# Fifteen input loads of an attention-and-feed-forward kernel, issued by ScalarE instead of SyncE

## The chip, the cores and the metric

The kernel runs on one core of a Trainium2 chip. The core has a matrix engine (TensorE, PE in the profile, with its weight loads as PEld), a vector engine (VectorE, DVE), a scalar engine (ScalarE, ACT), a general engine (GpSimd, POOL) and an engine that issues transfers and synchronizes (SyncE, SP). Each works through a queue of its own in order, and instructions wait for each other by semaphores. Sixteen DMA engines move data between HBM and the on-chip memory SBUF; TensorE's results land in PSUM, which has eight banks. The metric is the device time of one execution in microseconds; less is better.

## The reference

Eight batches of attention with 8 heads, 576 tokens and a head width of 64, of the kind that multiplies k by v first, so that no matrix of tokens by tokens arises; then a feed-forward layer with a product in the middle. All inputs and the output are in float32.

```python
q_s = softmax(q over the head width)
k_s = softmax(k over the 576 tokens)
kv  = einsum('bhsd,bhse->bhde', k_s, v)
x   = einsum('bhsd,bhde->bhse', q_s, kv)       # to (4608, 512)
h   = (x @ w1) * (x @ w2)                      # 512 -> 1024
out = (h @ w3) @ w_out                         # 1024 -> 1024 -> 512
```

In both softmaxes the greatest value is subtracted before the exponential, and 1e-9 is added to the sum.

## The kernel before

A class `Plan` holds some hundreds of named steps. A step has an engine (or several to choose from), a function that emits its instructions, and its needs. The text `ORDER` (from L83) lists the names by hand, and the steps are emitted in that sequence: each engine's queue is the sequence of its own steps in `ORDER`, and a letter behind a name (/A, /D, /P) picks ACT, DVE or POOL where there is a choice. Semaphores are set by what a step reads and overwrites. So `ORDER` says only what stands ahead of what on one engine; between engines the data decide.

At the start w3 @ w_out is folded to one matrix W3O of 1024 x 512 (L398). Then the work runs over batches b = 0 to 7 of attention and chunks c = 0 to 8 of the feed-forward layer, and the steps of several of them are interleaved so that PE has products of one while the other engines prepare the next. The steps for attention, with the lines at which the profile shows them:

- `q.b`, `k.b`, `v.b`: the loads (L358), from batch 2 on one transfer of 1152 KB each, all in float32. Each of the three has two buffers, which the batches use in turn, so that a load has to wait for the last step that reads the older batch in its buffer: the exponential of k two batches before for `k.b`, the exponential of q for `q.b`, the cast of v for `v.b`. The loads of batches 0 and 1 and of the weights are issued by POOL (two of q by SP); those of batches 2 to 7 by SP.
- `qmx` (DVE, L547: the maximum), `qsub` (POOL or DVE, L553), `qexp` (ACT, L561, into eq), `qsm` (DVE, L579: the sum), `qeps` and `qrc` (L585 and L590), `qn` (POOL, L597, into en): the softmax of q, in two parts p = 0 and 1 of each batch.
- `qd.b.p` (SP, L631): DMA transposes of a part of en to qT, as PE needs the head width in the partitions. Part 0 has 8 blocks, part 1 has 10.
- `kmi`, `kmx`, `cb` (ACT and DVE, L435 to L468): the maximum of k over the tokens; `ksub` (L475) and `kexp` (ACT, L483, into ek).
- `vc` (ACT, L275): the cast of v to float16. `kv` (PE, L501, into the banks pkv): k times v; `kv2` (DVE, L521 to L531): its division by the sums.
- `xm` and `xt` (PE, L649): q times kv, of the main 512 tokens and of the tails; `xs` and `xts` (mostly ACT, L279): their results, scaled and cast to the tiles x and xtail.

For a chunk: `up` (PE, L809, into pab: w1 and w2 side by side), `bs` (ACT, L275: one of them cast to bsb), `ab` (DVE, L834: the product), `down` (PE, L842, into po), `os` (ACT, L275, to outs) and `st` (SP, L869 and L969: the store). Chunk 8 collects the tails of all batches. Chunks 5 to 8 of the upward and 3 to 7 of the downward product are made with seven products in place of eight (steps um and dm, L904 and L945), with sums made by DVE and POOL.

On SP, loads, transposes and stores thus share one queue, in the sequence of `ORDER`; a step waits there for its needs, and everything behind it waits as well. An engine that issues a DMA goes on as soon as the issue is done; the transfer then runs by itself, and signals a semaphore when it lands. ACT issues only one transfer before the change, a part of the last store.

Of the kernel before, what the change touches and what calls it, by code (L numbers as in the profile page):

```python
# [101 lines left out]
up.1.1.1.3 qn.2.1/P kexp.2.0 down.1.0.0 down.1.0 kmi.3 kmx.3.0 bs.1.1.1/A ab.1.1.1 vc.2.0/A qd.2.0 xt.1 bs.1.1.2/A
ksub.2.1/P vc.2.1/A kmx.3.1 cbt.3 kexp.2.1 qsub.3.1/P xts.1.0/A ab.1.1.2 xts.1.1/A q.4 qexp.3.1 ws.2.0/P ab.1.1.0 kv.2
kv2.2 down.1.1.0 down.1.1 qd.2.1 xm.2.1 qmx.3.0 qsub.3.0/P os.1.0/A bs.1.1.3/A xs.2.1.1/A qmx.4.1 qsub.4.1/P xm.2.0
xs.2.0.1/A xt.2 qsm.3.1 xs.2.0.0/A xs.2.1.0/A cbx.3 xts.2.1/A v.3 down.1.2.0 up.0.1.1.3 up.1.2.0.0 bs.2.0.0/A qmx.4.0
xts.2.0/D up.0.2.0.0 up.1.2.0.1 qsub.4.0/P up.0.2.0.1 up.1.2.0.2 k.4 v.4 qexp.3.0 cb.3 ksub.3.1/P qsm.3.0 os.1.1/A
# [5 lines left out]
qrc.4.0 qn.4.0/P cbt.4 cbx.4 kv.3 ab.2.0.7 qexp.5.0 down.2.0 kv2.3 xm.3.0 xs.3.0.1/A xs.3.0.0/A xm.3.1 xs.3.1.0/A xt.3
xts.3.1/A xts.3.0/A cb.4 ksub.4.1/P k.5 qmx.6.1 down.2.1 xs.3.1.1/D qsm.5.0 vc.4.1/A os.2.1/A ksub.4.0/P up.1.3.0.0
up.0.3.0.0 qmx.6.0 qsub.6.0/P bs.3.0.0/A ab.3.0.0 os.2.0/A qeps.5.0/A qrc.5.0 st.1.1 qmx.5.1 qsub.5.1/P up.1.3.0.1
up.0.3.0.1 up.1.3.0.2 up.0.3.0.2 bs.3.0.1/A qd.4.1 up.1.3.0.3 up.0.3.0.3 up.1.3.0.4 ab.3.0.1 v.5 kmi.5 kmx.5.0 kmx.5.1
cbt.5 st.2.1 kexp.4.0 vc.4.0/A kexp.4.1 kv.4 bs.3.0.2/A qsub.6.1/P kv2.4 bs.3.0.4/A up.0.3.0.4 ab.3.0.4 down.2.2
bs.3.0.3/A ab.3.0.2 qexp.5.1 qd.4.0 cbx.5 qsm.5.1 qexp.6.0 xm.4.1 xs.4.1.0/A xm.4.0 xs.4.0.1/A qn.5.0/P xs.4.0.0/A
up.1.3.0.5 ws.3.1/D up.0.3.0.5 up.1.3.0.6 up.0.3.0.6 v.6 qeps.5.1/A wt.4/D ws.4.0/D os.2.2/A wt.3/D ws.3.0/D qrc.5.1
qn.5.1/P qexp.6.1 cb.5 ksub.5.0/P bs.3.0.6/A ab.3.0.6 k.6 vc.5.0/A xs.4.1.1/A up.1.3.0.7 up.0.3.0.7 q.7 qsm.6.1
ab.3.0.3 bs.3.0.5/A vc.6.0/A up.1.4.0.0 ab.3.0.5 up.0.4.0.0 up.1.4.0.1 st.1.3 bs.3.0.7/A ksub.5.1/P up.0.4.0.1 qsm.6.0  # L120
kmi.6 bs.4.0.1/A bs.4.0.0/A kmx.6.0 st.2.0 vc.6.1/A down.2.3 qeps.6.1/A os.2.3/A qrc.6.1 kmx.6.1 up.1.4.0.2 qd.5.0
# [8 lines left out]
ue.5.1.2/A k.7 xs.6.0.1/A ad.4.2/D um.5.2.6 ue.5.2.2/A ad.4.4/D um.5.1.7 ws.4.1/D um.5.2.7 ue.5.2.7/A um.5.0.7  # L130
um.5.1.5 ue.5.1.4/A ue.5.1.7/A ad.4.3/D um.5.2.2 uc.5.2.1 qeps.7.0/A um.5.0.1 xs.6.0.0/A um.5.2.4 uc.5.2.3 qrc.7.0
ue.5.0.7/A um.5.1.3 uc.5.1.4/P ab.5.1.1 ue.5.0.1/A um.5.2.5 ue.5.2.4/A um.5.1.2 uc.5.1.1 ab.5.2.0/P st.3.0 st.2.2
um.5.0.2 uc.5.0.1 um.5.0.4 um.5.0.6 ue.5.0.2/A uc.5.0.3 uc.5.2.4/P um.5.3.7 xd.6.3/P qn.7.0/P dm.4.1 kmi.7 kmx.7.0
um.5.3.1 ue.5.3.7/A um.5.1.4 uc.5.1.3 ab.5.1.0/P kmx.7.1 ue.5.3.1/A um.5.3.2 uc.5.3.1 de.4.1/A um.5.0.5 ue.5.0.4/A
# [1048 lines left out]
```

## Time and profile before

| | |
|---|---|
| median of 3 runs | 227.42 us (227.4 to 227.42) |
| profiled execution | 227.57 us |
| its span, first to last instruction | 225.8 us |
| granted TensorE clock | 1.000 |
| PE busy | 219.3 us, 97% |
| PE's weight loads busy | 150.6 us, 67% |
| DVE busy | 203.9 us, 90% |
| ACT busy | 161.6 us, 72% |
| POOL busy | 141.1 us, 62% |
| moved by DMA | 46.89 MB, 208 GB/s over the span |

A busy share says how much of the span an engine worked, not what it cost. Here PE is the engine to watch: where it is never idle, work on the others lies beside it and costs nothing until it comes too late for a product. For that, the rows of the instructions in order of time are read, with their start and length: how long before its use a tile was ready. A wait is put down to the semaphore that came last. A DMA has two times: the issue, in which the issuing engine's queue is held, and the landing. In the tables of DMA queues q1 is SP's ring, q0 is POOL's.

### The profile page before, as it was taken

The page shows a single profiled execution, that of the slowest core. Times are in us where ns is not written, and L with a number is a line of the kernel's source. Part 1 is how long each engine was busy: PE and PEld are TensorE (multiplying, and loading weights), DVE is VectorE, ACT ScalarE, POOL GpSimd, SP SyncE. Part 2 cuts the span into 40 slices and gives each one's busy share as a digit, 9 for nine tenths or more (in the row PEclk, how much of TensorE's full clock was granted, in tenths as well). Part 3 has the DMA queues.
Part 4 walks back from the last instruction along what each step waited for, and adds up shares of the span by engine and source line. Part 5 has one row for each costly group of instructions (what it writes and reads, how often), then busy time and mean ns, then how long its engine had stood idle before and what let it go on. Part 6 is the DMA issues. An engine that isn't in the chain of part 4 may idle for free.

```text
span 225.8 us, 5662 instructions
## 1 busy us (share of the span) xinstructions
PE 219.3 (97%) x2250; PEld 150.6 (67%) x2250; DVE 203.9 (90%) x363; ACT 161.6 (72%) x280; POOL 141.1 (62%) x96
## 2 busy tenths in 40 slices
PE   7998999999999999999999999999999999999994
PEld 2454658865886544444444657888888888888853
DVE  2989879989998999999998999999999988899881
ACT  2556476785859997899999986988995846453511
POOL 8344405787999799999679928297474055602320
PEclk9999999999999999999999999999999999999999
DMA  6999999999999999999969186482193040044343
GB/s 222 214 273 248 294 227 251 367 387 300 277 276 369 388 324 357 187 312 280 385 164 296 22 134 212 128 221 96 32 200 64 3 107 34 3 124 157 89 145 139
DMA packets 38042, 46.89 MB, mean 208 GB/s; under 512 B 18048, under 2 KB 21504, under 8 KB 38016
## 3 DMA queue, kind: packets, MB, share of 16 engines
q1 hardware_dynamic: 32144, 35.92, 56.5%
q0 software_dynamic: 5728, 10.55, 20.0%
q8 instruction: 17, 0.28, 0.5%
q10 hardware_dynamic: 144, 0.07, 0.1%
q14 instruction: 9, 0.07, 0.1%
HBM read 38.80 MB, written 9.44 MB: 214 GB/s over the span
## 4 chain that ended last, share of the span: by engine, by line
PE 67%; DMA 20%; DVE 8%; ACT 2%; POOL 1%; issue 1%; POOLq 0%; ACTq 0%; SPq 0%; DVEq 0%
PE pab L809 19%; PE uA L904 12%; PE dA L945 8%; DMA w1sb<-in_moe_w_dram 8%; PE uB L904 6%; PE po L842 6%; DMA w<-in_moe_w_dram 5%; DMA wosb<-in_moe_w_out_dram 5%; PE dB L945 4%; DMA q<-in_q_dram 3%; PE uC L904 3%; PE po L857 3%; PE dC L945 2%; DVE qm L547 2%; PE pkv L501 2%; DVE qr L579 2%
## 5 line engine op out<-in xcount | busy, mean ns | idle before, releaser
L809 PE MATMUL pab<-x,w2sb 128*128 128x256 f16 (+1 forms) x224 | 40.6, 318 | 0.0
L809 PE MATMUL pab<-x,w1sb 128*128 128x256 f16 (+1 forms) x224 | 40.6, 318 | 0.0
L597 POOL TENSOR_TENSOR en<-eq,qr 128x1024 f16<-128x1024 f16 (+1 forms) x14 | 29.7, 2126 | 8.3 <-DVE k L475 4.3
L809 PEld LDWEIGHTS <-w2sb 128*128 128x128 f16 x224 | 21.6, 98 | 13.4 <-issue 1.0
L809 PEld LDWEIGHTS <-w1sb 128*128 128x128 f16 x224 | 21.7, 98 | 13.0 <-issue 0.2
L553 POOL TENSOR_TENSOR q<-q,qm 128x1280 f32<-128x1280 f32 (+1 forms) x13 | 27.7, 2143 | 2.2 <-DVE qm L547 1.8
L475 POOL TENSOR_TENSOR k<-k,cb 128x1152 f32<-128x1152 f32 x10 | 26.2, 2626 | 2.5 <-DVE k L475 2.5
L904 PEld LDWEIGHTS <-w 128*128 128x128 f16 x256 | 25.0, 98 | 3.3
L834 DVE TENSOR_TENSOR ab<-pab,bsb 128x512 f16<-128x512 f32 x40 | 25.9, 672 | 0.2
L275 ACT CAST bsb<-pab 128x512 f16<-128x512 f32 x40 | 23.2, 594 | 3.8 <-PE pab L809 3.6
L561 ACT ACTIVATE eq<-q 128x1024 f16<-128x1024 f32 (+2 forms) x16 | 18.7, 1169 | 8.2 <-DVE q L553 7.6
L547 DVE TENSOR_REDUCE qm<-q 128x16 f32<-128x1024 f32 (+2 forms) x16 | 21.2, 1333 | 3.7 <-DMA q<-in_q_dram 3.7
L842 PE MATMUL po<-W3O,ab 128*128 128x512 f16 x96 | 22.7, 380 | 0.0
L579 DVE TENSOR_REDUCE qr<-eq 128x16 f32<-128x1024 f16 (+2 forms) x16 | 21.4, 1339 | 0.0
L483 ACT ACTIVATE ek<-k 128x1152 f16<-128x1152 f32 x16 | 18.8, 1172 | 3.3 <-DVE k L475 2.4
L279 ACT ACTIVATE x<-xm 128x512 f16<-128x512 f32 x30 | 16.4, 605 | 3.6 <-PE xm L649 1.9
L904 PE MATMUL uA<-v,w 128*128 128x256 f16 x128 | 17.9, 273 | 0.0
L275 ACT COPY v<-uA 128x512 f32<-128x512 f32 x24 | 14.1, 601 | 4.8 <-PE uA L904 4.3
L945 PEld LDWEIGHTS <-k 128*128 128x128 f16 x160 | 15.5, 98 | 2.1
L883 POOL TENSOR_TENSOR k<-ab,k 128x1024 f16<-128x1024 f16 x3 | 6.4, 2130 | 16.4 <-DVE bsb L883 10.0
L275 ACT CAST v<-v 128x1152 f16<-128x1152 f32 x14 | 16.3, 1170 | 0.0
L398 PE MATMUL pf<-wosb,aux 128*128 128x512 f16 x64 | 15.6, 379 | 0.4 <-DMA wosb<-in_moe_w_out_dram 0.4
(140 smaller groups left out, 464.7 us busy)
## 6 DMA issues: line engine op xcount, KB each, us to landing
q<-in_q_dram SPq DMA_DIRECT2D x6, 1152.0 KB, 6.5
k<-in_k_dram SPq DMA_DIRECT2D x6, 1152.0 KB, 8.9
v<-in_v_dram SPq DMA_DIRECT2D x6, 1152.0 KB, 8.8
out_dram<-outs SPq DMA_DIRECT2D x23, 256.0 KB, 3.5
...
```

The costliest lines, as they stand in the source:

```text
L275: return [(nc.scalar.copy if eng == "ACT" else engine[eng].tensor_copy)(out=out, in_=in_)]
L475: return [engine[eng].tensor_tensor(out=kb[:, two(hp), :, :], in0=kb[:, two(hp), :, :], in1=st["cb", b][:, two(hp), None, :].broadcast_to( ...
L483: nc.scalar.activation(out=st["ek", b][:, hp, :, :].rearrange("p j (i d) -> p i j d", i=2), in_=kb[:, two(hp), :, :], func=AF.Exp)
L547: dve.tensor_reduce(out=st["qm", b][:, hs, j], in_=qb[:, hs, j, :], axis=AX.X, op=ALU.max, **({"negate": True} if (b, p) in FEXP else {}))
L553: return [engine[eng].tensor_tensor(out=qb[:, hs, j, :], in0=qb[:, hs, j, :], in1=st["qm", b][:, hs, j, None].broadcast_to([P, nh, n, D]), ...
L579: dve.tensor_reduce(out=st["qr", b][(slice(None), *part(p))], in_=st["eq", b, p], axis=AX.X, op=ALU.add)
L597: return [engine[eng].tensor_tensor(out=st["en", b][:, j, hs, :].rearrange("p j h d -> p h j d"), in0=st["eq", b, p], in1=st["qr", b][:, h ...
L809: nc.tensor.matmul(st["p", one, c, sub, u][:, a * (t1 - t0):(a + 1) * (t1 - t0)], lhsT=w[:, ct, fb * P:(fb + 1) * P], rhs=x()[:, ct, t0:t1 ...
L834: dve.tensor_tensor(out=st["ab", c][:, nf * u:nf * u + nf, t0:t1], in0=cut(st["p", 0, c, sub, u]), in1=cut(st["bsb", c, sub, u]), op=ALU.mult)
L842: nc.tensor.matmul(st["po", c, tb], lhsT=st["ab", c][:, ft, tb * P:(tb + 1) * P], rhs=W3O[:, ft, :], start=(ft == 0), stop=(ft == N_FT - 1))
L904: nc.tensor.matmul(t[:, u, :], lhsT=w[:, k0 + kk, fb * P:(fb + 1) * P], rhs=r[:, kk, :], start=(p in (1, 2, 7) and u == 0 and kk == 0), st ...
L945: nc.tensor.matmul(t[:, i, :], lhsT=l[:, f, i * P:(i + 1) * P], rhs=r[:, f, :], start=(p in (1, 2, 7) and i == 0 and f == 0), stop=(i == 1 ...
```

## The change

The loads of q, k and v of batches 3 to 7 are issued by ACT instead of SP. A list of names picks them; the loads of batch 2, the transposes and the stores stay on SP. In `ORDER` the moved loads get places among ACT's steps, about where SP came to issue them, and a few steps of SP (qd.2.0, qd.2.1, qd.4.0, qd.4.1, qd.6.1, st.1.1, st.2.2, st.3.0) stand a little earlier. The computing instructions of ACT, PE, DVE and POOL stand in the same sequence as before. What a load waits for is the same as before; only that the wait now stands in ACT's queue.

```diff
@@ ORDER
-up.0.0.1.3 ab.0.0.2 k.3 ab.0.1.0 bs.0.1.3/A ab.0.1.3 ws.1.1/D up.0.0.1.2 bs.0.1.2/A ab.0.1.2 down.0.0.0 qmx.2.0
+up.0.0.1.3 ab.0.0.2 ab.0.1.0 bs.0.1.3/A ab.0.1.3 ws.1.1/D up.0.0.1.2 bs.0.1.2/A ab.0.1.2 down.0.0.0 qmx.2.0 down.0.0
...
+    ALOAD = [('q', 3), ('q', 4), ('q', 5), ('q', 6), ('q', 7), ('k', 3), ('k', 4), ('k', 5), ('k', 6), ('k', 7), ('v', 3), ('v', 4), ('v', 5), ('v', 6), ('v', 7)]
...
     for b in range(2, B):
         for n in "kqv":
-            load((n, b), "SP")
+            load((n, b), "ACT" if (n, b) in ALOAD else "SP")
```

Three places show what that makes of the queues. In the names, q32_1, k32_1 and v32_1 are the second buffers of the inputs (batches 1, 3, 5) and q32_0, k32_0 and v32_0 the first ones. First SP's queue between 42 and 57 us, from q.2 to v.2, before and after:

```order
L358 DMA q32_0_71<-in_q_dram 128x4x576
L358 DMA k32_0_69<-in_k_dram 128x4x576
L631 DMA_TRANSPOSE qT_710<-en_688 128x8x128
L358 DMA k32_1_70<-in_k_dram 128x4x576
L358 DMA q32_1_72<-in_q_dram 128x4x576
L631 DMA_TRANSPOSE qT_710<-en_688 128x10x128
L358 DMA v32_0_73<-in_v_dram 128x4x576
```

```order
L359 DMA q32_0_71<-in_q_dram 128x4x576
L359 DMA k32_0_69<-in_k_dram 128x4x576
L632 DMA_TRANSPOSE qT_710<-en_688 128x8x128
L632 DMA_TRANSPOSE qT_710<-en_688 128x10x128
L359 DMA v32_0_73<-in_v_dram 128x4x576
```

k.3 and q.3 stood between the two transposes of batch 1 and are gone from there. Second, ACT's queue at the casts of v of batch 1, around 46 to 53 us, before and after:

```order
L275 CAST bsb_686<-pab_676 128x512
L275 CAST bsb_713<-pab_541 128x512
L275 CAST bsb_737<-pab_716 128x512
L275 CAST bsb_750<-pab_666 128x512
L275 CAST v16_1_76<-v32_1_74 128x2x9x64 x2
L561 ACTIVATE eq_775<-q32_1_72 128x1280
L585 ACTIVATE qr_636<-qr_636,epst_79 128x4x5
```

```order
L276 CAST bsb_686<-pab_676 128x512
L276 CAST bsb_713<-pab_541 128x512
L276 CAST bsb_736<-pab_716 128x512
L276 CAST bsb_749<-pab_666 128x512
L359 DMA k32_1_70<-in_k_dram 128x4x576
L276 CAST v16_1_76<-v32_1_74 128x2x9x64 x2
L562 ACTIVATE eq_775<-q32_1_72 128x1280
L359 DMA q32_1_72<-in_q_dram 128x4x576
L586 ACTIVATE qr_636<-qr_636,epst_79 128x4x5
```

k.3 now stands ahead of the casts of v, and q.3 right behind the exponential of q that last reads its buffer. Third, ACT's queue around 70 to 73 us, at the exponential of k of batch 2, before and after:

```order
L275 CAST v16_0_75<-v32_0_73 128x2x9x64
L483 ACTIVATE ek_1106<-k32_0_69 128x2x9x64
L279 ACTIVATE xtail_80<-xt_1127 128x2x64
L279 ACTIVATE xtail_80<-xt_1128 128x2x64
L561 ACTIVATE eq_1155<-q32_1_72 128x1280
```

```order
L276 CAST v16_0_75<-v32_0_73 128x2x9x64
L359 DMA v32_1_74<-in_v_dram 128x4x576
L484 ACTIVATE ek_1110<-k32_0_69 128x2x9x64
L359 DMA k32_0_69<-in_k_dram 128x4x576
L359 DMA v32_0_73<-in_v_dram 128x4x576
L280 ACTIVATE xtail_80<-xt_1129 128x2x64
L280 ACTIVATE xtail_80<-xt_1130 128x2x64
L562 ACTIVATE eq_1159<-q32_1_72 128x1280
```

v.3 stands ahead of that exponential, k.4 and v.4 directly behind it; k.4 overwrites the buffer that it reads.

More of the change, by code (lines that the diff above doesn't have):

```diff
@@ L102 @@
[L102 to L106, printed above, removed]
@@ L112 @@
[L112 to L116, printed above, removed]
@@ L117 @@
[L117 to L121, printed above, removed]
@@ L122 @@
-qn.6.1/P qeps.6.0/A qrc.6.0 qn.6.0/P up.0.4.0.2 ab.4.0.0 up.1.4.0.3 bs.4.0.2/A ab.4.0.2 up.0.4.0.3 up.1.4.0.4
+qn.2.0/P qd.2.0 wt.2/P up.1.1.0.1 up.0.1.0.1 bs.1.0.1/A qexp.2.1 kmx.2.1 up.1.1.0.2 cb.2 bs.1.0.2/A ksub.2.0/P
+up.0.1.0.2 up.1.1.0.3 os.0.0/A os.0.1/A xm.1.1 q.4 xs.1.1.1/A qsm.2.1 xs.1.1.0/D ab.1.0.1 qeps.2.1/A qrc.2.1 ab.1.0.0
+bs.1.0.3/A up.0.1.0.3 up.1.1.1.0 up.0.1.1.0 up.1.1.1.1 qmx.3.1 up.0.1.1.1 ab.1.0.3 ab.1.0.2 bs.1.1.0/A up.1.1.1.2
+up.0.1.1.2 up.1.1.1.3 qn.2.1/P qd.2.1 kexp.2.0 down.1.0.0 down.1.0 kmi.3 kmx.3.0 bs.1.1.1/A ab.1.1.1 vc.2.0/A xt.1
@@ new lines @@
+bs.1.1.2/A ksub.2.1/P vc.2.1/A kmx.3.1 cbt.3 v.3 kexp.2.1 qsub.3.1/P k.4 v.4 xts.1.0/A ab.1.1.2 xts.1.1/A qexp.3.1
+ws.2.0/P ab.1.1.0 kv.2 kv2.2 down.1.1.0 down.1.1 xm.2.1 qmx.3.0 qsub.3.0/P os.1.0/A bs.1.1.3/A xs.2.1.1/A qmx.4.1
+qsub.4.1/P xm.2.0 xs.2.0.1/A xt.2 qsm.3.1 xs.2.0.0/A xs.2.1.0/A cbx.3 xts.2.1/A down.1.2.0 up.0.1.1.3 up.1.2.0.0
+bs.2.0.0/A qmx.4.0 xts.2.0/D up.0.2.0.0 up.1.2.0.1 qsub.4.0/P up.0.2.0.1 up.1.2.0.2 qexp.3.0 cb.3 ksub.3.1/P qsm.3.0
+os.1.1/A up.0.2.0.2 ab.1.1.3 up.1.2.0.3 q.5 qeps.3.1/A qrc.3.1 qn.3.1/P bs.2.0.1/A st.1.0 qexp.4.1 qsm.4.1 bs.2.0.2/A
@@ new lines @@
+xs.3.0.0/A xm.3.1 xs.3.1.0/A xt.3 xts.3.1/A xts.3.0/A cb.4 ksub.4.1/P qmx.6.1 down.2.1 xs.3.1.1/D qsm.5.0 vc.4.1/A
+os.2.1/A ksub.4.0/P up.1.3.0.0 up.0.3.0.0 qmx.6.0 qsub.6.0/P bs.3.0.0/A ab.3.0.0 os.2.0/A qeps.5.0/A qrc.5.0 qmx.5.1
+qsub.5.1/P up.1.3.0.1 up.0.3.0.1 up.1.3.0.2 up.0.3.0.2 bs.3.0.1/A up.1.3.0.3 up.0.3.0.3 up.1.3.0.4 ab.3.0.1 kmi.5
+kmx.5.0 kmx.5.1 cbt.5 st.2.1 qd.4.0 kexp.4.0 vc.4.0/A kexp.4.1 kv.4 v.6 bs.3.0.2/A qsub.6.1/P kv2.4 k.6 bs.3.0.4/A
+up.0.3.0.4 ab.3.0.4 down.2.2 bs.3.0.3/A ab.3.0.2 qexp.5.1 cbx.5 qsm.5.1 qexp.6.0 xm.4.1 xs.4.1.0/A xm.4.0 xs.4.0.1/A
@@ new lines @@
+qn.5.0/P xs.4.0.0/A up.1.3.0.5 ws.3.1/D up.0.3.0.5 up.1.3.0.6 up.0.3.0.6 qeps.5.1/A wt.4/D ws.4.0/D os.2.2/A wt.3/D
+ws.3.0/D qrc.5.1 qn.5.1/P qexp.6.1 cb.5 ksub.5.0/P bs.3.0.6/A ab.3.0.6 q.7 vc.5.0/A xs.4.1.1/A up.1.3.0.7 up.0.3.0.7
+qsm.6.1 ab.3.0.3 bs.3.0.5/A vc.6.0/A up.1.4.0.0 ab.3.0.5 up.0.4.0.0 up.1.4.0.1 st.1.3 bs.3.0.7/A ksub.5.1/P up.0.4.0.1
+qsm.6.0 kmi.6 bs.4.0.1/A bs.4.0.0/A kmx.6.0 st.2.0 vc.6.1/A down.2.3 qeps.6.1/A os.2.3/A qrc.6.1 kmx.6.1 up.1.4.0.2
+qd.5.0 qn.6.1/P qeps.6.0/A qrc.6.0 qn.6.0/P up.0.4.0.2 ab.4.0.0 up.1.4.0.3 bs.4.0.2/A ab.4.0.2 up.0.4.0.3 up.1.4.0.4
@@ L130 @@
[L130 to L134, printed above, removed]
@@ new lines @@
+um.5.1.1 ue.5.1.1/A ue.5.2.1/A xm.6.0 xd.5.4/D xt.6 xts.6.0/A ad.4.1/D dm.3.3 xts.6.1/A dc.3.2/A st.3.0 st.2.2
+um.5.1.6 xd.5.1/D dc.3.4/D ue.5.1.2/A xs.6.0.1/A ad.4.2/D um.5.2.6 ue.5.2.2/A ad.4.4/D um.5.1.7 ws.4.1/D um.5.2.7
+ue.5.2.7/A um.5.0.7 um.5.1.5 ue.5.1.4/A ue.5.1.7/A ad.4.3/D um.5.2.2 uc.5.2.1 v.7 qeps.7.0/A um.5.0.1 xs.6.0.0/A
+um.5.2.4 uc.5.2.3 qrc.7.0 ue.5.0.7/A um.5.1.3 uc.5.1.4/P ab.5.1.1 ue.5.0.1/A um.5.2.5 ue.5.2.4/A um.5.1.2 uc.5.1.1
+ab.5.2.0/P um.5.0.2 uc.5.0.1 um.5.0.4 um.5.0.6 ue.5.0.2/A uc.5.0.3 uc.5.2.4/P um.5.3.7 xd.6.3/P qn.7.0/P dm.4.1 kmi.7
@@ new lines @@
+kmx.7.0 um.5.3.1 ue.5.3.7/A um.5.1.4 uc.5.1.3 ab.5.1.0/P kmx.7.1 ue.5.3.1/A um.5.3.2 uc.5.3.1 de.4.1/A um.5.0.5
+ue.5.0.4/A uc.5.0.4/P um.5.3.6 xd.6.2/P ue.5.3.2/A dm.4.6 um.5.2.3 ab.5.2.1 um.6.0.1 qexp.7.1 qsm.7.1 cbt.7 um.5.3.5
+ue.5.3.4/A dm.4.2 xd.6.1/D dm.4.7 um.6.2.1 um.5.0.3 um.5.3.3 dc.4.1 ab.5.0.1 vc.7.1/A um.5.3.4 uc.5.3.3 uc.5.3.4/P
+ab.5.0.0/P de.4.7/A dm.4.4 st.3.1 qeps.7.1/A qrc.7.1 ue.6.0.1/A ab.5.3.1 um.6.0.6 ab.5.3.0/P um.6.0.7 cbx.7 cb.7
+de.4.2/A dc.4.3 xd.6.4/D ue.6.0.2/A ue.6.0.7/A ue.6.2.1/A dm.4.5 de.4.4/A dc.4.4/D um.6.0.5 ue.6.0.4/A uc.6.0.4/D
@@ new lines @@
+st.4.1 um.6.1.1 ue.6.1.1/A um.6.2.7 ue.6.2.7/A dm.4.3 dc.4.2/A um.6.3.1 ue.6.3.1/A um.6.0.4 um.6.3.7 ue.6.3.7/A
+um.6.0.2 ksub.7.1/D ksub.7.0/D qd.7.0 qn.7.1/P kexp.7.1 um.6.1.6 um.6.3.6 um.6.2.6 ue.6.2.2/A uc.6.0.3 uc.6.0.1
+ab.6.0.0/P um.6.3.4 vc.7.0/A um.6.2.4 uc.6.2.3 um.6.0.3 ab.6.0.1 um.6.2.2 uc.6.2.1 um.6.1.2 uc.6.1.1 um.6.1.7 um.6.3.2
+uc.6.3.1 ab.6.2.0/P um.6.2.5 ue.6.3.2/A um.6.3.5 uc.6.3.3 kexp.7.0 ue.6.2.4/A ad.5.1/D uc.6.2.4/D dm.5.1 kv.7
+ue.6.1.2/A ad.5.2/D ue.6.3.4/A uc.6.3.4/P um.6.1.5 um.6.2.3 kv2.7 st.4.0 ue.6.1.7/A um.6.1.4 de.5.1/A uc.6.1.3
@@ new lines @@
+ab.6.2.1 dm.5.2 um.6.3.3 ab.6.3.1 ue.6.1.4/A dc.5.1 dm.5.6 de.5.2/A um.6.1.3 qd.7.1 xm.7.1 xm.7.0 xs.7.0.0/A
+xs.7.0.1/A xs.7.1.1/A xt.7 uc.6.1.4/P dm.5.5 ad.5.3/D ad.5.4/D dm.5.7 um.7.2.1 ab.6.3.0/D ab.6.1.1 xts.7.1/A
+xs.7.1.0/A um.7.1.1 xd.7.3/D xd.7.2/D xd.7.4/D ad.6.1/D um.7.3.1 de.5.7/A xd.7.1/D dm.5.4 dc.5.3 ue.7.1.1/A xts.7.0/D
+um.7.1.6 um.7.1.2 uc.7.1.1 ab.6.1.0/P ue.7.2.1/A um.7.2.6 um.7.1.7 de.5.4/A dc.5.4/P ue.7.1.2/A ue.7.1.7/D um.7.1.5
+dm.6.2 um.7.2.7 ue.7.3.1/D um.7.3.2 uc.7.3.1 um.7.1.4 uc.7.1.3 st.5.1 ue.7.1.4/A uc.7.1.4/P um.7.1.3 ab.7.1.1 ad.6.2/D
@@ new lines @@
+ue.7.2.2/A um.7.2.5 um.7.3.6 ue.7.2.7/A ue.7.3.2/D um.7.3.7 um.7.2.4 uc.7.2.3 ue.7.2.4/A uc.7.2.4/P um.7.0.1
+ue.7.0.1/A dm.5.3 dc.5.2/A um.7.2.2 ad.6.3/D um.7.0.7 xd.8.3/D ab.7.1.0/D um.7.2.3 ab.7.2.1 um.8.1.1 uc.7.2.1 um.7.3.5
+ad.6.4/P ue.7.3.7/A um.7.3.4 uc.7.3.3 ab.7.3.0/D um.7.0.6 dm.6.1 ue.7.0.7/A um.7.0.2 ue.7.3.4/A uc.7.0.1 xd.8.2/P
+um.7.0.4 ue.7.0.2/A uc.7.0.3 ab.7.0.0/P dm.6.7 de.6.1/A dc.6.1 de.6.7/A uc.7.3.4/D dm.6.6 um.7.0.5 ue.7.0.4/A
+uc.7.0.4/D ue.8.1.1/A um.7.3.3 um.8.0.7 st.2.3 um.8.0.1 um.7.0.3 ue.8.0.1/D xd.8.4/P de.6.2/A ab.7.0.1 dm.6.4 dc.6.3
```

45 lines of the change are left out of this document (11 added, 34 removed).

## The prediction

> **What bounds the kernel now.** I read the page first: shares of busy time and the span in 40 slices.
>
> ```profile
> PE 219.3 (97%) x2250; PEld 150.6 (67%) x2250; DVE 203.9 (90%) x363; ACT 161.6 (72%) x280; POOL 141.1 (62%) x96
> ...
> ACT  2556476785859997899999986988995846453511
> ...
> DMA  6999999999999999999969186482193040044343
> ```
>
> PE is busy for 219.3 of 225.8 us. A slice is 5.6 us: the DMA engines are full from the second slice to the twentieth (6 to 112 us), and ACT, at 72% on average, stands at 9 in that same stretch. So the loads are moved onto an engine that is nearly full there, while the wires that they use are full too. The busy time by stage (columns: us, then busy us of PE, PE's weight loads, DVE, ACT and POOL; then granted clock, share of the DMA engines, GB/s):
>
> ```profile
> 45.00:55.00 10.00, 10.00 (x135) 5.82 (x133) 9.14 (x17) 7.39 (x11) 8.28 (x5) 1.00 1.10 338
> 55.00:65.00 10.00, 9.73 (x90) 7.85 (x89) 9.58 (x22) 7.04 (x14) 9.60 (x5) 1.00 1.11 322
> 65.00:75.00 10.00, 9.88 (x147) 6.83 (x148) 9.06 (x19) 8.65 (x13) 9.51 (x5) 1.00 1.13 317
> 75.00:125.00 50.00, 50.00 (x404) 23.35 (x396) 48.70 (x86) 46.50 (x84) 45.67 (x21) 1.00 1.00 292
> 125.00:145.00 20.00, 20.00 (x309) 13.77 (x308) 19.64 (x40) 17.36 (x36) 10.97 (x6) 1.00 0.52 116
> 145.00:219.00 74.00, 74.00 (x739) 64.35 (x737) 68.40 (x120) 47.88 (x89) 35.83 (x27) 1.00 0.40 104
> ```
>
> From 45 to 219 us PE is idle for 0.27 + 0.12 = 0.39 us, at a granted clock of 1.00 throughout. That is all a better order of loads can win there: the loads that move are issued from 49 us on, so the change can save at most 0.4 us, and whatever it makes late on PE is lost in full. The share of DMA over 1.00 only says that an engine has more than one packet in the air: in these stages the wires have no room.
>
> Next the chain that ended last (start, us, what), and PE's waits after 45 us:
>
> ```profile
> 42.10 7.75 DMA q<-in_q_dram
> 49.88 1.22 DVE qm L547
> ...
> 71.26 1.07 ACT ek L483
> 72.38 0.48 PE pkv L501 x36
> ```
>
> ```profile
> PE xm L649 <- DMA qT<-en: 0.3, 1, 0.3
> ```
>
> The chain runs through the load q.2, then DVE, then ACT's exponential of k of batch 2, and reaches PE at 72.38; from there PE runs on to the end. The only wait on PE with a name is for the transposes of q (step qd.1.1, below).
>
> **The change part by part.** First SyncE's queue (SP) as it was (start, us that the issue took):
>
> ```profile
> 42.58 0.44 SPq L358 DMA_DIRECT2D k<-in_k_dram  x1
> 45.59 3.56 SPq L631 DMA_TRANSPOSE qT<-en  x1
> 49.27 0.52 SPq L358 DMA_DIRECT2D k<-in_k_dram  x1
> 50.56 0.37 SPq L358 DMA_DIRECT2D q<-in_q_dram  x1
> 55.99 1.42 SPq L631 DMA_TRANSPOSE qT<-en  x1
> ...
> 72.35 0.37 SPq L358 DMA_DIRECT2D k<-in_k_dram  x1
> 72.77 0.50 SPq L358 DMA_DIRECT2D v<-in_v_dram  x1
> ...
> 135.57 0.40 SPq L358 DMA_DIRECT2D k<-in_k_dram  x1
> ```
>
> In order: k.2, qd.1.0, k.3, q.3, qd.1.1, then k.4 and v.4, and k.7 far behind. Behind SP nobody computes, so its issue times cost nothing; but its queue is a file, in which the transposes qd.1.0 stood ahead of k.3 and q.3. From issue to landing (tile qT: the one issue at 45.59, the one at 55.99, and all 14):
>
> ```profile
> DMA to landing us min/median/max: 8.2/8.2/8.2
> ...
> DMA to landing us min/median/max: 6.4/6.4/6.4
> ...
> DMA to landing us min/median/max: 3.7/4.9/8.2
> ```
>
> So qd.1.0 landed at 45.59 + 8.2 = 53.8. On PE (start, us, what, idle before in brackets):
>
> ```profile
> 51.94 1.90 PE L842 MATMUL po<-W3O,ab 128*128 128x512 f16 x8
> 53.80 0.41 PE L649 MATMUL xm<-qT,kv 64*64 64x256 f16 x8
> ...
> 62.42 0.41 PE L649 MATMUL xm<-qT,kv 64*64 64x256 f16 x8 [0.27 <-DMA qT<-en]
> ...
> 72.79 1.90 PE L842 MATMUL po<-W3O,ab 128*128 128x512 f16 x8
> ```
>
> The x of batch 1 (xm, 53.80) reads that tile at once, behind products that end at 53.8: the transposes come with no slack at all. Each microsecond that qd.1.0 lands later is one of PE. Now ACT, where the loads are put:
>
> ```profile
> 46.19 1.07 ACT L275 CAST bsb<-pab 128x512 f16<-128x512 f32 x2 [0.33 <-PE pab L809]
> 47.15 2.22 ACT L275 CAST v<-v 128x1152 f16<-128x1152 f32 x2
> 49.27 1.27 ACT L561 ACTIVATE eq<-q 128x1280 f16<-128x1280 f32 x1
> 52.52 0.31 ACT L585 ACTIVATE qr<-qr,epst 128x20 f32<-128x20 f32 x1 [1.99 <-DVE qr L579]
> ...
> 71.15 1.17 ACT L483 ACTIVATE ek<-k 128x1152 f16<-128x1152 f32 x1
> 72.22 0.45 ACT L279 ACTIVATE xtail<-xt 128x128 f16<-128x128 f32 x2
> ```
>
> *k.3, and with it qd.1.0 (term D).* On ACT, k.3 stands between the two bsb casts that end at 47.26 and the casts of v, so it is issued by 47.26, two microseconds before SP's 49.27, and on a ring of its own: it no longer stands behind qd.1.0. How long an issue takes to its first packet, two views of DMA show, k.7 alone on idle wires and the window that I need below (40 slices each, 0.05 and 0.115 us):
>
> ```profile
> DMA  0000000000000000000000779854124599592993
> ```
>
> ```profile
> q1 hardware_dynamic: 103, 0.24, 63.5%
> q0 software_dynamic: 43, 0.14, 38.3%
> ```
>
> ```profile
> DMA packets 1532, 1.32 MB, mean 286 GB/s; under 512 B 1075, under 2 KB 1075, under 8 KB 1532
> ```
>
> k.7's first packets came 22 slices or 1.1 us behind its issue; behind a backlog it is longer. I take 49.1 for k.3 (between 48.4 and 49.8). The second fence, 44.6 to 45.6 us, shows what two rings with work do: SP's (q1) and GpSimd's (q0) shared the engines, 63.5% to 38.3%. The third, 48.8 to 53.4: 1.32 MB moved, 0.26 MB of it the 1024 transposes of 256 B, about 0.1 at the end k.3. Ahead of and between the transposes lay 0.96 MB of q.2 and k.2; by 49.1 another 0.12 (0.3 us at the 392 GB/s of the next row) is gone, and 0.84 MB or 2.1 us of loads are left.
>
> ```profile
> DMA packets 349, 0.78 MB, mean 392 GB/s; under 512 B 12, under 2 KB 12, under 8 KB 349
> ```
>
> That row is 46 to 48 us. With k.3's 1152 KB sharing half and half, these 2.1 us take 4.2: +2.1. The transposes themselves (50.6 to 53.2, 2.6 us) then meet the rest of k.3 and q.3, which ACT issues right behind its eq at 50.5. I take +1.0 for them: their 256-byte packets left the wires part empty in that window (286 GB/s), so a second ring costs them less than double. D = 3.1. From below it is 0 (k.3's packets come after the transposes anyhow); from above 6.0 (2.1 + 2.6 + 1.3 for the last packets). I stay in the middle because the one row on two rings is close to half and half.
>
> The Trainium skill (DMA: Bandwidth & Descriptors, section "Queues, rings and completion order") says that each DMA engine goes round the rings that it has work for, a packet at a time; the row of 44.6 to 45.6 agrees, with its 63.5 to 38.3. The same page ("Issuing engines are not separate DMA queues") says that issuing from several engines only saves issue time, and it speaks against the change: no row here shows issue time on SP that anyone waits for. By an even split for the transposes too, D would be 4.7 and the sum below 1.6 higher.
>
> q.2's tail is slowed as well, by up to 0.8 us (49.1 to 49.88), and DVE's qm with it. But PE is then already late by D, and DVE's chain meets PE only at 72.38; the two run side by side, and only the larger counts. The waits of 0.27 and 0.12 us at 62.4 and 72.3 fall into the shift: -0.2, as new ones need not be smaller.
>
> *q.3* on ACT follows eq, in front of 1.99 us of idle: 0. *q.4* lies where ACT idles for x: 0. With q.4, k.3 and q.3 gone, SP's own transposes (qd.1.1, qd.2.x) have less ahead of them; they share wires instead, 0.
>
> *v.3* stands between a cast of v and ek of batch 2 (71.15 in the row above), the instruction of the chain. An issue took 0.37 to 0.52 us in the rows of SP. If ACT computes ahead of it, 0; if it stops, 0.42. I take 0.2.
>
> *k.4 and v.4* follow ek directly, and k.4 overwrites what ek reads: it waits for ek's end (72.32), then 0.37 + 0.50 of issues and gaps; the next work starts at about 73.27 instead of 72.22: +1.05. Behind it stand the two pieces of xtail (0.45 together, the first over by about 72.5), whose PSUM bank PE's po takes at 72.79, so 0.29 of the delay is slack. Cost 0.8, from 0 (the queue runs on) to 1.05. Who waits: PE for the bank, DVE for the eq behind it.
>
> *q.5, q.6, k.5, v.5, v.6, k.6, q.7* lie between 80 and 115 us, where ACT is busy for 46.50 of 50. Seven issues by 0.42 are 2.9 us, against 3.5 us of idle time, most of it in places where the issue doesn't fall. q.5, q.6, k.5, k.6 and q.7 come one short instruction behind the end of the one that they wait for. From 0 to 2.9; I take 0.4, since in this stage PE is never idle and each of its products is then some tenths ahead or behind. *k.7 and v.7* lie after 125 us, where ACT has 2.6 us free of 20: 0.
>
> The sum: 227.57 (the profiled execution, span 225.8) + 3.1 - 0.2 + 0.2 + 0.8 + 0.4 = 231.9. It stands 0.15 above the median of 227.42, so the median after is about 231.7.
>
> **The rivals.** *The generator is shared.* SP's issue of qd.1.0 took 3.56 us, to 49.15. If a second queue's issue cannot start until that is over, ACT stands still from 47.26 to 49.15 with v and eq behind it: eq 2.4 us late with its own issue, DVE's reduction after it, kv of batch 1 1.6 us late at xm (53.80); then k.3 comes at about 49.7, shares little, and D is about 0.5. 227.57 + 1.6 + 0.5 + 1.1 of ACT's gaps - 0.15 = 230.6. For it: the one long issue in the table, its others being 1.42 and less. Against it: no row has two queues issuing at once. The same page's passage on HWDGE ordering says that SP and ACT have no descriptor generator of their own; no run of this case shows yet what that does to an issue.
>
> *Only ACT's gaps.* The rings do not hurt the transposes (small packets fit in between); then 227.57 + 0.2 + 0.8 + 0.4 - 0.2 - 0.15 = 228.6. For it: 286 GB/s while the transposes ran; against it, the split of 44.6 to 45.6.
>
> *The freed file (the other side).* In before, qd.1.1 took 6.4 us and PE waited 0.27 for it, behind k.3 and q.3. Without them it would take the 3.7 of the smallest row and land at 59.7: PE's 0.39 us of waits go, 227.42 - 0.35 = 227.1. It decides if k.3's first packets come after 53.2, or q.2's and k.2's do not share, and ACT goes past its issues without a stop. Against it: k.3 is issued two microseconds earlier than before.
>
> *ACT becomes the bound.* Fifteen issues by 0.42 are 6.3 us, against 3.5 idle in 75 to 125; if each stops ACT for its whole issue, PE waits for bsb and x again and again: 227.4 + 3.1 + 2.5 to 4.5, 233 to 235. For it: the 46.50 of 50; against it, that q.3, q.4, k.7 and v.7 fall into idle time.
>
> **How the numbers follow.** The forecast (D about 3, gaps about 1) has 46%, the shared generator 11%, only gaps 16%, the freed file 16%, ACT as the bound 11%. A measurement here can tell 0.2% or 0.45 us from no change. The freed file ends within it in 11 and beyond it in 5 of its 16; the others are slower by more. So faster 0.05, same 0.11, slower 0.84. The range goes from 227.7, which leaves out the freed file, to 235.0, where ACT is the bound: about 8 in 10.
>
> **What would show it.** D: the transposes issued at about 45.6 land at 56 to 58 instead of 53.8, and PE's xm of batch 1 waits some 3 us for qT. The gaps: an idle time of ACT of about 1 us before xtail near 75 us, and PE's po waiting for it. The shared generator: idle time on ACT before the casts of v at 47 us. The forecast is wrong if xm of batch 1 starts without a wait, or if PE's lost time lies mainly after 80 us.

## The result, and the profile after

The change makes the kernel slower by far more than the range allowed: 243.19 us median (242.09 to 246.59, four runs) against 227.42 (227.40 to 228.30). The profiled execution shown here took 246.59 us, the longest of the four, so its parts add up to 19 us and not to the 16 of the median. The ratio, 1.067 with a 95% interval of 1.064 to 1.071, leaves this execution out, as it lies more than 1.5% above the fastest.

PE's waits after 45 us in the profile after (us in total, times, longest):

```profile
PE xm L650 <- DMA qT<-en: 11.7, 1, 11.7
PE pab L810 <- ACT x L280: 2.0, 2, 1.3
PE xm L650 <- ACT bsb L276: 0.8, 2, 0.6
PE po L843 <- DVE ab L835: 0.5, 1, 0.5
```

The one named wait before, 0.3 us, was for qd.1.1. Now PE waits 11.7 us at the place that the prediction named: xm of batch 1 waits for the transposes qd.1.0. The busy time by stage (columns as before the change):

```profile
45.00:55.00 10.00, 8.80 (x121) 5.29 (x119) 9.08 (x17) 6.70 (x9) 8.21 (x5) 1.00 1.15 321
55.00:65.00 10.00, 0.00 (x0) 0.00 (x0) 6.28 (x16) 0.59 (x1) 9.59 (x5) 0.62 1.18 201
65.00:75.00 10.00, 9.48 (x60) 6.05 (x60) 0.17 (x1) 4.61 (x8) 0.30 (x1) 0.70 0.55 163
...
125.00:145.00 20.00, 17.14 (x81) 7.42 (x79) 17.09 (x29) 19.66 (x36) 12.05 (x6) 1.00 0.82 224
```

PE does nothing from 53.8 to 65.5. Two further losses stand in these rows. The granted clock is 0.62 and 0.70 around the idle time, and PE's first products behind it are slow: eight matmuls of po take 3.60 us where they took 1.90, and those of pab behind them 1.77 instead of 1.04.

```profile
65.52 0.64 PE L650 MATMUL xm<-qT,kv 64*64 64x256 f16 x8 [11.72 <-DMA qT<-en]
66.10 3.60 PE L843 MATMUL po<-W3O,ab 128*128 128x512 f16 x8
69.49 1.77 PE L810 MATMUL pab<-x,w2sb 128*128 128x256 f16 x8
71.10 1.04 PE L810 MATMUL pab<-x,w1sb 128*128 128x256 f16 x8
```

And between 125 and 145 us PE is idle for 2.9 us, in a stage in which ACT is busy throughout, as if ACT had come late to it. The page gives the balance:

```profile
span 244.8 us, 5647 instructions
...
PE 223.7 (91%) x2250; PEld 151.9 (62%) x2250; DVE 204.7 (84%) x363; ACT 162.4 (66%) x280; POOL 141.1 (58%) x96
```

PE's idle time went from 225.8 - 219.3 = 6.5 to 244.8 - 223.7 = 21.1 us, 14.6 more, and its busy time from 219.3 to 223.7, 4.4 more for the same 2250 matmuls. Of these 4.4 the rows above show 2.7, behind the idle time at the low clock. Another 1.4 come between 122 and 135 us at a clock of 1.00: a matmul that starts behind a wait does not overlap with the one before it (the eight xm of batch 4 take 0.40, 0.40 and 0.89 us in three pieces, and took 0.63 in one).

### The profile page after: what moved, and what is told of

Read it like the earlier page. It is cut to its first block, busy times and chain, and to the rows that moved or that the text cites. A ratio compares the mean times of both kernels' runs of the same rounds, so it can differ in the third digit from the quotient of the medians.

```text
span 244.8 us, 5647 instructions
## 1 busy us (share of the span) xinstructions
PE 223.7 (91%) x2250; PEld 151.9 (62%) x2250; DVE 204.7 (84%) x363; ACT 162.4 (66%) x280; POOL 141.1 (58%) x96
## 4 chain that ended last, share of the span: by engine, by line
PE 60%; DMA 22%; ACT 7%; DVE 5%; issue 2%; POOL 2%; ACTq 1%; POOLq 0%; DVEq 0%
PE pab L810 15%; PE uA L905 12%; DMA qT<-en 8%; DMA w<-in_moe_w_dram 8%; PE dA L946 7%; DMA q<-in_q_dram 6%; PE po L843 6%; PE uB L905 6%; PE dB L946 4%; PE uC L905 3%; PE po L858 3%; ACT eq L562 2%; PE dC L946 2%; PE xm L650 2%; ACT bsb L276 1%
## 5 line engine op out<-in xcount | busy, mean ns | idle before, releaser
L810 PE MATMUL pab<-x,w2sb 128*128 128x256 f16 (+1 forms) x224 | 41.5, 323 | 2.4 <-ACT x L280 2.0
L843 PE MATMUL po<-W3O,ab 128*128 128x512 f16 x96 | 24.4, 400 | 0.7 <-DVE ab L835 0.5
L650 PE MATMUL xm<-qT,kv 64*64 64x512 f16 (+1 forms) x80 | 7.0, 360 | 12.6 <-DMA qT<-en 11.7
L843 PEld LDWEIGHTS <-ab 128*128 128x128 f16 x96 | 9.3, 101 | 11.9 <-issue 2.5
## 6 DMA issues: line engine op xcount, KB each, us to landing
w<-in_moe_w_dram POOLq DMA_DIRECT2D x8, 256.0 KB, 11.7
```

The lines of the kernel that those rows point to most:

```text
L810: nc.tensor.matmul(st["p", one, c, sub, u][:, a * (t1 - t0):(a + 1) * (t1 - t0)], lhsT=w[:, ct, fb * P:(fb + 1) * P], rhs=x()[:, ct, t0:t1 ...
L843: nc.tensor.matmul(st["po", c, tb], lhsT=st["ab", c][:, ft, tb * P:(tb + 1) * P], rhs=W3O[:, ft, :], start=(ft == 0), stop=(ft == N_FT - 1))
```

## The experiments

**k.3 and q.3 back on SP.** The thirteen other loads stay on ACT.

```diff
-ab.0.0.2 ab.0.1.0
+ab.0.0.2 k.3 ab.0.1.0
...
-down.0.1 k.3 vc.1.1/A
+down.0.1 vc.1.1/A
...
-qsm.1.1 q.3 qeps.1.1/A
+qsm.1.1 qeps.1.1/A
...
-kv.1 kv2.1
+kv.1 q.3 kv2.1
...
-    ALOAD = [('q', 3), ..., ('k', 3), ...]
+    ALOAD = [('q', 4), ('q', 5), ('q', 6), ('q', 7), ('k', 4), ('k', 5), ('k', 6), ('k', 7), ('v', 3), ('v', 4), ('v', 5), ('v', 6), ('v', 7)]
```

> The changed kernel with k.3 and q.3 back on SP, at the places that they had before; the other thirteen loads stay on ACT. Theory 'two rings': transposes on SP's ring and loads on ACT's ring hold each other up while both are in flight, and the wait of 11.7 us for qd.1.0 with the low clock behind it is the bulk of the loss. Then qd.1.0 lands at about 53.8 again, PE's wait at xm of batch 1 is gone, and what is left is the 2.9 us at 125 to 145 and some tenths: 229.5 to 232. Rival 'ACT': the issues in ACT's queue and what they wait for cost most, so thirteen of fifteen loads keep most of the loss: 237 or more.

Measured: 233.01 us, ratio 1.023 (1.019 to 1.027). Ten of the sixteen microseconds are gone with these two loads, and the clock in the profile is 1.00 throughout. But 5.4 are left, more than "two rings" allowed; the longest wait is no longer that of xm of batch 1.

**k.3 and q.3 alone on ACT.** The kernel before, with two names in `ALOAD`, and these two at their changed places in `ORDER`.

> The kernel before with k.3 and q.3 alone on ACT, at the places that they have after the change. 'Two rings': PE waits about 11 us for qd.1.0 at xm of batch 1 and runs at a lower clock for some us behind it: 238 to 241. 'ACT': two issues, one ahead of idle time, cost under 1 us: 227.5 to 228.5.

Measured: 241.29 us, ratio 1.059 (1.055 to 1.063). Two loads make 13.7 of the 15.6 us. (With the 5.4 that the other thirteen cost by themselves, that is more than the whole. Presumably what else is late costs less behind a wait of 11 us; no run shows it.) PE waits 11.4 us, and the landing of qd.1.0, 8.2 us behind its issue before, is now (tile qT, the issue at 45.4):

```profile
DMA to landing us min/median/max: 19.4/19.4/19.4
```

**The sequence alone.** The changed `ORDER` with `ALOAD = []`.

> The changed kernel's ORDER with every load on SP: the steps of SP that were moved in ORDER, without any load on ACT. Both theories: one ring, k.3 and q.3 behind qd.1.0 as before, 227.2 to 228.5. A third, 'the sequence on SP', that the moved steps of SP alone make something late, would give more than 230.

Measured: 227.66 us against 227.59, ratio 1.000 (0.999 to 1.002). The moved steps of SP cost nothing.

**k.3 alone on ACT.**

> The kernel before with k.3 alone on ACT; q.3 stays on SP behind qd.1.0. Rival 'bytes': the wires are shared and always full, so qd.1.0 can be later by at most k.3's own 1152 KB, 3.0 us at 390 GB/s, and the time is at most 230.5. 'Two rings': the two kinds of packets slow each other beyond their bytes; k.3 has half the bytes that held qd.1.0 up by 11.7 us, so 5 to 6 us of wait and about 1 us of lower clock, 233 to 235.

Measured: 235.23 us, ratio 1.031 (1.026 to 1.036). qd.1.0 lands 14.3 us behind its issue, at 60.2; PE waits 6.1 (the view names a DVE step as the releaser, but xm starts at 60.20, right behind the landing). The delay of 6.4 is twice what k.3's bytes can fill at 390 GB/s, so "bytes" falls.

**k.3 and q.3 on a third ring.** The kernel before, with these two issued by POOL, at places among POOL's steps.

```diff
-            load((n, b), "SP")
+            load((n, b), "POOL" if (n, b) in ALOAD else "SP")
```

> The kernel before with k.3 and q.3 on POOL's queue, k.3 behind the first en of batch 1 and q.3 behind the sum of weights at 48.7 to 50.8 us: the same time as on ACT, but on a third ring. 'Two rings': whichever ring carries the loads, their packets and the transposes hold each other up; PE waits 6 to 12 us for qd.1.0: 234 to 242. Rival 'SP and ACT share a generator', that the harm is in two issues of these two engines at the same time (SP's issue of qd.1.0 took 5.7 us instead of 3.6): no such wait, and POOL's two issues cost 1 to 3 us: 228 to 230.5.

Measured: 239.77 us, ratio 1.052 (1.048 to 1.056). PE waits 10.7 us:

```profile
PE xm L650 <- DMA qT<-en: 10.7, 1, 10.7
```

The harm does not lie in ACT, nor in two issues that SP and ACT make at the same time. It came on both of the other rings that were tried, when loads that stood behind the transposes in SP's ring were put there.

**Packets of half the size.** k.3 and q.3 on ACT, each as two transfers that halve the run of 576 numbers.

```diff
-            st[name] = {...}[queue].dma_start(out=dst, in_=src)
+            n = dst.shape[-1] // (2 if name in ALOAD else 1)
+            for x in range(0, dst.shape[-1], n):
+                st[name] = {...}[queue].dma_start(out=dst[:, :, x:x + n], in_=src[:, :, x:x + n])
```

> The kernel before with k.3 and q.3 on ACT, each as two transfers with packets of 1152 bytes instead of 2304: the same bytes in twice as many packets. Theory 'turns': the rings take turns by packets, the 1024 transposes need 1024 turns and so let 1024 load packets past, 2.4 MB as they are; with half the size they let 1.2 MB past, so qd.1.0 lands some 3 us earlier than the 64.7 of the same kernel with whole packets: 237 to 239. Theory 'standstills': the time goes in stretches in which nearly nothing moves, as transposes wait for each other; packet size changes little or makes it worse: 240 to 243.

Measured: 234.56 us, ratio 1.031 (1.030 to 1.033). The same bytes on the same ring, and more than half of the loss is gone: qd.1.0 lands 13.3 us behind its issue, at 58.8 instead of 64.7, and PE waits 5.1. The size of the gain is beyond what "turns" gave, its direction is against "standstills".

**Packets of a quarter, for k.3 alone.** The same with four transfers, and q.3 on SP.

> The kernel before with k.3 alone on ACT, as four transfers with packets of 576 bytes: 2048 packets in place of 512. 'Turns': the 1024 transposes of qd.1.0 let 1024 of these past, half of k.3 (0.6 MB) instead of all of it; qd.1.0 then lands at 56.5 to 58.5, before k.3 has landed, instead of 60.2, and the time is 230.5 to 233. 'Standstills' alone: more packets mean more meetings, and qd.1.0 lands at 60 or later: 235 or more.

Measured: 230.32 us, ratio 1.012 (1.010 to 1.014). qd.1.0 lands 10.4 us behind its issue, at 55.9, a little earlier than "turns" gave, and PE waits 0.9 for it. (Four issues in a row also hold ACT, and PE waits 1.3 us for a cast of v: the time is not lost at the transposes alone.)

What the rings do can be counted. Packets, MB and share on ACT's ring (q10) and SP's (q1): from 50.2 to 52.2 us with k.3 and q.3 whole on ACT, from 50.2 to 52.2 with k.3 in quarters, and from 53.5 to 56.5 with both in halves, when SP's ring held hardly anything but transposes (0.21 MB in 801 packets); last POOL's ring (q0) and SP's from 49.5 to 53.0 us in the run on the third ring, where POOL's load packets are of 4608 bytes and those of SP of 2304:

```profile
q10 hardware_dynamic: 193, 0.44, 78.1%
q1 hardware_dynamic: 192, 0.33, 63.9%
```

```profile
q1 hardware_dynamic: 315, 0.38, 97.2%
q10 hardware_dynamic: 322, 0.19, 78.8%
```

```profile
DMA packets 1602, 1.12 MB, mean 372 GB/s; under 512 B 831, under 2 KB 1600, under 8 KB 1600
...
q10 hardware_dynamic: 799, 0.89, 82.3%
q1 hardware_dynamic: 801, 0.21, 30.0%
```

```profile
q0 software_dynamic: 195, 0.90, 67.0%
q1 hardware_dynamic: 198, 0.46, 36.0%
```

The packets are shared one to one, whatever their size; the bytes are not (0.90 to 0.46 MB), nor is the engines' time (67.0% to 36.0%). A transposition of 256 bytes takes one turn, and so does a load packet of 2304. The Trainium skill (DMA: Bandwidth & Descriptors, section "Queues, rings and completion order") says that an engine goes round its rings by packets, and these rows agree, 799 to 801. So the 1024 transposes of qd.1.0 let as many load packets past as there are, up to about 1024 (reckoned, not counted; about, as the engines do not keep step: where one is through with its loads, transposes follow each other there):

| loads on ACT, packet | load packets let past | MB | at 392 GB/s, us | qd.1.0 later by, us |
|---|---|---|---|---|
| k.3 and q.3, 2304 bytes | 1024 | 2.36 | 6.0 | 10.9 |
| k.3, 2304 bytes | 512 (all) | 1.18 | 3.0 | 6.4 |
| k.3 and q.3, 1152 bytes | 1024 | 1.18 | 3.0 | 5.0 |
| k.3, 576 bytes | 1024 | 0.59 | 1.5 | 2.1 |

(The landings 64.7, 60.2, 58.8 and 55.9 less 53.8.) The delay goes by the bytes that are let past, and is 1.4 to 2.1 times what they take at the full rate. The rest is a lower rate. The wires from 50.5 to 55.0 us in the kernel with k.3 and q.3 on ACT (40 slices of 0.11 us):

```profile
DMA  9999999899999999899992333233323339621112
GB/s 369 430 348 369 430 389 430 330 394 396 357 421 362 351 369 391 303 284 278 173 166 102 143 123 143 102 143 123 127 107 148 127 130 107 105 105 66 71 68 89
DMA packets 569, 1.07 MB, mean 237 GB/s; under 512 B 118, under 2 KB 118, under 8 KB 569
```

From the time that transposes are among the packets, the rate falls here from about 390 to 100 GB/s. Taking turns alone does not do that: in the stretch with halves above, the two rings took turns one to one at 372 GB/s. In the packet records of the change, transposes that usually take 0.02 us take 1 to 3.3 us and end together, at 55.2, 57.7 and 64.1, and at the first two of these times load packets of the other ring end with them. The kernel before has such stretches too, one for qd.1.0 with 16 transposes of 0.9 to 1.57 us that end at 52.6 to 52.7, and others for the transposes behind it. I read this as transposes that wait for each other across the DMA engines and hold the loads in the engines meanwhile, but no run here separates that from other reasons.

**v.6 on SP as well.** Most of what is left with k.3 and q.3 on SP is in ACT's queue. In that experiment ACT, busy all around, stops for 4.2 us at v.6 (ACT, start, us, idle before):

```profile
105.53 1.16 ACT L484 ACTIVATE ek<-k 128x1152 f16<-128x1152 f32 x1
110.51 0.38 ACTq L359 DMA_DIRECT2D v<-in_v_dram  x1
110.93 0.58 ACT L276 CAST bsb<-pab 128x512 f16<-128x512 f32 x1 [4.24 <-DMA qT<-en]
```

In the program, the DMAs of SP and ACT use eight semaphores in turn, in the sequence of `ORDER`, and each waits until the one eight before it has landed. ACT's queue after the change, at v.6, with the semaphores:

```
127 L484 ACTIVATE ek_1721<-k32_0_69 128x2x9x64 [waits Pool_49]
128 L276 CAST v16_0_75<-v32_0_73 128x2x9x64
129 L484 ACTIVATE ek_1721<-k32_0_69 128x2x9x64
130 L359 DMA v32_0_73<-in_v_dram 128x4x576 [waits DMAHW2_49,Activation_49]
131 L276 CAST bsb_1800<-pab_1678 128x512 [waits PE_49]
```

DMAHW2 is the semaphore of the transposes qd.4.0. After the change these landed at 124.56 and v.6 was issued at 124.63; ACT had been idle since 120.3. With k.3 and q.3 on SP, they landed at 110.44 and v.6 was issued at 110.51. (The 109.4 and 14.9 us in the expectation that follows are those of qd.4.1, which was issued at 94.5.) On SP such a wait holds up nobody who computes.

> As the experiment with k.3 and q.3 on SP, and v.6 back on SP as well (it stays at its place in ORDER, and waits there on SP). There ACT stood for several us at v.6's issue, since v.6 signals the same semaphore as the transposes qd.4.0 and may not start until these have landed (109.4, behind 14.9 us of transposes mixed with v.5). Theory 'ACT waits for a landing': PE's 2.6 us of idle time at 105 to 125 us go in the main, 229.5 to 231. Rival 'late transposes alone': x of batch 4 is late whatever ACT does, since qd.4.1 and qd.4.0 still land at about 109: 232 to 233.5, as with v.6 on ACT.

Measured: 232.37 us, ratio 1.020 (1.014 to 1.025), within the error of the kernel with v.6 on ACT, and in the range of "late transposes alone". The stop at v.6 is gone, but another has come:

```profile
117.40 0.38 ACTq L359 DMA_DIRECT2D q<-in_q_dram  x1
117.82 1.15 ACT L276 CAST v<-v 128x1152 f16<-128x1152 f32 x1 [2.26 <-DMA k<-in_k_dram]
```

As v.6 moved, the turn of the semaphores moved with it, and q.7 now waited for k.6 to land. This run tells the theories apart badly.

**k.6 and q.7 on SP, too.** Ten loads on ACT.

> The changed kernel with k.3, q.3, v.6, k.6 and q.7 on SP and ten loads on ACT. With v.6 alone moved, ACT's stop had gone from v.6 to q.7, whose issue now waited until k.6 had landed (117.32) on the same semaphore, and PE idled 2.0 us. Theory 'ACT waits for a landing': with neither k.6 nor q.7 on ACT, PE's idle time at 105 to 125 us goes, and what is left is 0.3 at 55 to 65 and 1.2 at 65 to 85: 228.3 to 229.5. Rival 'late transposes alone': qd.4 still meets v.5, 230.5 or more.

Measured: 229.33 us, ratio 1.007 (1.005 to 1.009). By stage:

```profile
55.00:65.00 10.00, 9.75 (x88) 7.63 (x87) 9.58 (x22) 7.28 (x14) 9.59 (x5) 1.00 1.12 325
65.00:85.00 20.00, 18.80 (x204) 11.61 (x202) 18.11 (x30) 17.22 (x30) 18.60 (x10) 1.00 1.08 344
85.00:105.00 20.00, 20.00 (x176) 9.23 (x174) 19.76 (x37) 17.91 (x34) 19.07 (x10) 1.00 1.07 262
105.00:125.00 20.00, 20.00 (x167) 9.03 (x166) 19.09 (x37) 19.39 (x34) 16.60 (x8) 1.00 1.03 275
```

PE has no idle time at 105 to 125 us, though v.5 and the transposes of batch 4 still meet. So "ACT waits for a landing" holds: of the 3.7 us between 233.01 and 229.33, 2.6 are idle time that PE had in this stage with v.6, k.6 and q.7 on ACT (17.42 us busy of 20), and has no longer. What is left is 1.2 us at 65 to 85.

**Five loads in the clear.** k.4, v.4, q.5, k.7 and v.7 on ACT, the rest as before.

> The kernel before with k.4, v.4, q.5, k.7 and v.7 on ACT, at the places that they have after the change; the other loads on SP. These five meet few transposes: those of batch 2 are down by 72.6, those of batch 3 start at 86.9. 'Two rings', with issues on ACT hidden behind the work that its sequencer has queued ahead: 227.2 to 228.0. By the terms of the prediction k.4 and v.4 cost 0.8 and the others some tenths: 228.2 to 228.6.

Measured: 228.00 us against 227.55, ratio 1.0021 (1.0012 to 1.0031), between the two. ACT at k.4 and v.4, and PE behind it:

```profile
71.14 1.17 ACT L484 ACTIVATE ek<-k 128x1152 f16<-128x1152 f32 x1
72.34 0.43 ACTq L359 DMA_DIRECT2D k<-in_k_dram  x1
72.80 0.53 ACTq L359 DMA_DIRECT2D v<-in_v_dram  x1
73.38 0.45 ACT L280 ACTIVATE xtail<-xt 128x128 f16<-128x128 f32 x2 [1.06 <-PE pkv L502]
```

```profile
73.31 1.89 PE L843 MATMUL po<-W3O,ab 128*128 128x512 f16 x8 [0.46 <-DVE ab L835]
...
76.00 1.02 PE L843 MATMUL po<-W3O,ab 128*128 128x512 f16 x4 [0.18 <-ACT bsb L276]
```

The row of xtail names PE as the releaser, but it starts 0.05 us behind v.4's issue: ACT lost 1.06 us there, and PE 0.46 and 0.18 of them. The loads in the clear cost 0.45 us in all, about what a measurement can tell; none of them waits for a landing, and qd.1.0 is untouched.

**q.3 behind qd.1.1 on SP.** Could another sequence win what the kernel before leaves, 0.39 us of PE's waits?

```diff
-kv.1 q.3 kv2.1
+kv.1 kv2.1
...
-qn.1.1/P qd.1.1 qmx.2.1
+qn.1.1/P qd.1.1 q.3 qmx.2.1
```

> All loads on SP as before, with q.3 behind the transposes qd.1.1 in SP's queue instead of ahead of them. qd.1.1 has k.3 alone ahead of it and should land before 62.4, so that PE's waits of 0.27 and 0.12 us may go: 227.0 to 227.5, the most that the order of the loads can win here. Rival: q.3, now issued at about 57.5, lands after 65 and DVE's maximum of it is late: 227.6 to 229.

Measured: 227.99 us against 227.41, ratio 1.0013 (0.9998 to 1.0028): no difference that can be told, and no gain. No kernel that was run is faster than the kernel before.

## Why the prediction was wrong, step by step

*The bound, and the place of the loss: right.* PE had no slack at xm of batch 1, k.3 on a ring of its own made qd.1.0 late, and the wait appeared where it was foretold.

*Term D, 3.1 us with an upper bound of 6.0: wrong, 11.7.* Its first part, +2.1 for the loads ahead of the transposes, came near: k.2 landed at 55.2 instead of 52.9 (42.70 + 12.5 against 42.58 + 10.3), 2.3 later. That is luck in part: k.3's first packets came at 49.9, later than the 48.4 to 49.8 allowed, and so met less of q.2 and k.2, but at a falling rate. The step that failed is the second part, the +1.0 for the transposes: "their 256-byte packets left the wires part empty in that window, so a second ring costs them less than double". From k.2's landing to that of qd.1.0 it took 0.9 us before and 10.3 after, 9.4 more. This step, like the 4.7 beside it, took the wires to be split about evenly. The row on which the split rested, 63.5% to 38.3% at 44.6 to 45.6 us, does not show turns: it has 103 packets to 43, as POOL's ring was running out (28 of its packets in the first half, 15 in the second), and its shares are of engine time. Rings with work share by packets, one to one, and the small packet is the loser: every transposition of 256 bytes lets one load packet past that is nine times as large. In these units the transposes go at a tenth of the bytes, and last until both loads are through. That gives 6.0 us at the full rate; the wires, at 199 GB/s from 51.3 to 65.4, did not have it, which makes the rest. That view of the DMA engines after the change:

```profile
DMA packets 2871, 2.80 MB, mean 199 GB/s; under 512 B 1863, under 2 KB 1863, under 8 KB 2869
```

The prediction saw the 286 GB/s of the window with transposes in the kernel before, and took the empty part for room. It was part of what the transposes cost.

The smaller guesses in the same step held or did not matter: ACT issued k.3 at 46.07, before the 47.26 that was its bound, and q.2 landed at 49.9, not held up.

*The clock: left out.* No term stood for what a long wait does to PE behind it. The clock in the profile after (columns as above, the clock third from the end):

```profile
53.80:57.30 3.50, 0.00 (x0) 0.03 (x1) 3.36 (x5) 1.05 (x2) 3.09 (x2) 1.00 1.00 167
57.40:65.50 8.10, 0.00 (x0) 0.00 (x0) 4.02 (x13) 0.00 (x0) 7.90 (x4) 0.50 1.15 194
65.50:70.90 5.40, 5.38 (x23) 2.43 (x23) 0.00 (x0) 1.08 (x2) 0.00 (x0) 0.50 0.69 239
```

Half the clock is granted from 3.5 us into the wait until 5.4 us behind its end, and 5.4 us at half the clock are the 2.7 us of busy time. The Trainium skill (TensorE: Matmul & The Clock Gate, section "What's actually happening") says that the engine falls back to half its clock after an idle window of about 3.4 us; the rows agree, with 3.60 us instead of 1.90 behind 11.7 us of idle time. In the runs with waits of 5 to 11 us the mean of the granted clock in the ten microseconds from 55 falls to 0.54 (k.3 and q.3 on ACT) to 0.66 (halves); with waits of about 1 us it stays at 1.00.

*k.4 and v.4, 0.8 us (0 to 1.05): right.* With the five loads in the clear, ACT lost 1.06 us and PE 0.64.

*v.3, 0.2 us (0 to 0.42): 0.* The issue stood ahead of ek in the queue, and went out three microseconds before ek began, while a bsb cast ran (82.23 against 85.10). This issue waited for nothing on its own engine, and was made ahead of time. q.3, q.4, k.7 and v.7 at 0 held too, as far as ACT's time goes.

*The seven loads from 80 to 115 us, 0.4 (0 to 2.9): the size lies at the upper bound, for another reason.* Not their issue times, but v.6's wait for the landing of the transposes qd.4.0 on its semaphore: 4.3 us of ACT and 2.9 of PE. The step that failed counted, of what a load waits for, only the reader of its buffer. Its row among the semaphores was there to be read before the run.

*The rivals.* The shared generator falls: k.3 was issued by ACT at 46.07 in 0.48 us, in the midst of SP's issue of qd.1.0 (45.61 to 51.32), and POOL's ring did the same harm. That issue of SP took 5.71 us instead of 3.56, but it was over 14 us before the landing. Why k.3's first packets came 3.9 us behind its issue, and k.7's on idle wires 1.1, no run shows. Only gaps, the freed file and ACT as the bound fall with the traces.
